# Dilated window attention with a mixture of experts on one core: where the mask's second half is loaded, three gathers instead of two at an early table, and two weight sums placed later

## The chip, the core and the metric

The kernel runs on one core of one Trainium2 chip. A core has a matrix engine (TensorE, here PE, with its weight loads shown as PEld), a vector engine (DVE), a scalar engine (ACT), a general engine (GpSimd, here POOL) and a sync engine (SyncE, here SP) that issues most of the DMA transfers. Sixteen DMA engines move the data. The metric is the device time of one execution in microseconds (us), as the median of several runs.

## The reference

Attention with a window of 32 keys for the first four heads and with 32 keys at a distance of 4 (positions 0, 4, 8, ... back) for the last four, on 8 batches, 8 heads, 576 positions and 64 features. Its output, with the heads side by side, is a token matrix of 4608 tokens by 512. Each token then goes to one of 8 experts:

```python
logits = np.einsum('bsd,de->bse', x, w_gate)
local_gate = 1.0 / (1.0 + np.exp(-np.einsum('bsd,de->bse', x, w_local).squeeze(-1)))
...
        if s == 0 or local_gate[b, s] < 0.5:
            e = fresh_e
        else:
            e = prev_e if prev_e >= 0 else fresh_e
...
        h = np.maximum(x[b, s] @ w1[e], 0.0)
        out[b, s] = p[e] * (h @ w2[e])
```

A token takes the expert with the largest logit, or the expert of the token before it where its locality gate is at least 0.5. Weights are 512 x 1024 and 1024 x 512 per expert, in 32-bit floats.

## The kernel before

**Attention.** The 64 pairs of batch and head are taken two at a time: 32 head pairs, numbered n, and their loads come for two head pairs at once, numbered m = n // 2 (16 of them). `kq` holds keys and queries of an m, `vt` its values with a column of ones. For each n, `scores(n)` computes on PE, for blocks of 64 queries, the products with the 96 keys they can see, into a score bank of which there are two; DVE (line 332) limits them from below and takes the minimum with the mask `mk`; ACT (line 335) takes the exponential. `values(n)` multiplies with `vt` on PE (line 380), and DVE divides by the sum that came out of the column of ones (lines 384 and 385), which gives `x`. `turn` transposes `x` for the router, `store` writes it to memory as `xd`, and `spread(m)` lets POOL copy the second half of a `vt` into place (line 274). The order in the loop over n is scores of n, then values of n - 1. Heads of the plain and of the dilated kind need different masks: the kind is `(n % 4) // 2`, so n = 0 and 1 use the first half of `mk`, n = 2 and 3 the second, and so on. Loads of an m are issued in the iteration n = 2(m - 2), once a buffer is free (three buffers each for `kq` and `vt`).

**Routing.** Tokens are routed in four groups of two batches. `route(g)` computes the group's logits and lays a list of small steps (expert chosen, carried from the token before, counted, position in the expert's list) into two queues, `waiting` and `behind`, from which `gap` takes one at each gap of the matrix work. After two groups an early table of tokens exists (`early_tokens`), after four the late one (`late_tokens`).

**Experts.** The work is a list of units. A pair unit has 256 tokens of one expert; units 0 and 1 use the early table, and the units from 2 on the late table. `gather(u)` lists the gathers that fetch a unit's token rows from `xd` (four for each of the units 0 to 3), `fetch` issues one: a small memset on DVE, then an indirect DMA from POOL. `turn_rows` transposes the rows, and the expert's two layers follow, `hidden(u)` and `output(u)`. A pair unit's layer is computed with seven products of quarter matrices instead of eight (unit 1's hidden layer excepted), for which DVE forms sums of the weights' quarters (`sums_of_weights`, lines 870 to 873 and 876 to 879), of token rows (`xc`) and of hidden values (`hc`). The seven products of a layer share three banks of partial sums; each is drained on ACT or DVE as it ends (`finish`, line 1119 for the second layer).

**What sets the order.** PE and DVE execute in the order in which the program writes their instructions. Work that is pushed into `soon` is taken from it one or two at a time by `work_gap`, once per product. The instructions of POOL and ACT are put in order by a planner, from the program and costs that it assumes. SP issues its transfers in the program's order and on one queue. A transfer on it carries one of eight semaphores in turn, so the ninth waits until the first has landed.

Of the kernel before, what the change touches and what calls it, by code (L numbers as in the profile page):

```python
# [12 lines left out]
BF16 = mybir.dt.bfloat16  # L13
# [3 lines left out]
Alu = mybir.AluOpType  # L17
# [6 lines left out]
B, H, S, DH = 8, 8, 576, 64  # L24
# [8 lines left out]
QB = 64  # L33
NB = S // QB
KW = QB + WIN
# [170 lines left out]
def whole(ctx, tc, exact, bad, qk, v, wgl, w1, w2, con, msk, qmk, out, cst, wg, ones):  # L206
    nc = tc.nc
    name = "exact" if exact else "plain"
# [17 lines left out]
    def room(to, i, name, shape):  # L226
# [8 lines left out]
    ins, work, xp, xtp = (attention.enter_context(tc.tile_pool(name=name, bufs=bufs))  # L235
                     for name, bufs in (("ins", 3), ("work", 3), ("xp", 3), ("xtp", 2)))
# [53 lines left out]

    load(0, "kq", 0)
    if not exact:
        mk = work.tile([KW, 2 * S], BF16, name="mk", bufs=1)
        nc.sync.dma_start(out=mk[:, :S], in_=msk[:, :S])
    else:
        qm = work.tile([P, QB + 2 * NB * KW], BF16, name="qm", bufs=1)
        nc.sync.dma_start(out=qm, in_=qmk)
# [5 lines left out]
    load(1, "vt")  # L303
    if not exact:
        nc.sync.dma_start(out=cst, in_=con)
        nc.sync.dma_start(out=mk[:, S:], in_=msk[:, S:])
    spread(0)


# [5 lines left out]
    def scores(n):  # L315

        kt, qt = keys(n)
        kind = (n % NP) // (NP // 2)
        prob[n] = []
        for part, (a, z) in enumerate(UNITS):  # L320
            w = (z - a) * QB
            sc = two("sc")
            for i in range(a, z):
                for u in range(2):
                    h = slice(u * DH, (u + 1) * DH)
                    nc.tensor.matmul(sc[:KW, u, (i - a) * QB:(i - a + 1) * QB], lhsT=kt[h, i * QB:i * QB + KW],  # L326
                                     rhs=qt[h, i * QB:(i + 1) * QB], start=True, stop=True,
                                     tile_position=(u * DH, 0))
            pr = prs[n % 2 * 2 + part]
            to = pr[:KW, :, :w]  # L330
            at = kind * S + a * QB
            nc.vector.scalar_tensor_tensor(  # L332
                to, sc[:KW, :, :w], -CEIL,
                mk[:, at:at + w].unsqueeze(1).to_broadcast([KW, 2, w]), Alu.max, Alu.min)
            nc.scalar.activation(to, to, Act.Exp, scale=SCALE)  # L335
            prob[n].append(pr)

# [369 lines left out]
    def table(late):  # L707

        cols = COLS if late else 2 * FIRST
        chosen = tiles["chosen", late]  # L710
        ep = bank([1, cols], "ep")
        for k, c in enumerate(chosen):
            nc.tensor.matmul(ep, lhsT=cst[:, C_E:C_UP], rhs=c[:, 0], start=(k == 0), stop=(k == len(chosen) - 1))
        tiles["experts", late] = experts = sm.tile([1, cols], I32, name="experts_late" if late else "experts_early")
        nc.vector.tensor_copy(experts, ep)
# [140 lines left out]
    def now(push):  # L856
        for f in push:
            f()
# [22 lines left out]
    def sums_of_weights(u, second):  # L881

        i = units[u]["slot"]
        assert (u, second) in loads
        if second:
            return sums_right(sums[1], *(quarter(raw2[i], k, j, True) for k in range(2) for j in range(2)))
        return sums_left(sums[0], *(quarter(raw1[i], f, k, False) for f in range(2) for k in range(2)))
# [242 lines left out]
    def route(g):  # L1130

        turned_back, first_best, owned, exponentials = fresh(g)
        before_it, lane_and_segment = place(g)
        lane0, lane1, segment, code, what = matrices(g)
        counts = count(g == NG - 1)

        def now(*fs):
            return [lambda: [f() for f in fs]]

        def of(*fs):  # L1140
            return [lambda: [f(g) for f in fs]]

        def sum_up():
            products(g, not g)

        def counted_on():
            next(counts)

        if g < NG - 1:
            logits(g)  # L1150
            if g == EARLY - 1:
                tail = (now(what) + now(counted_on) + now(sum_up, counted_on) + pause
                        + now(lambda: table(False), early_tokens))
            else:
                tail = now(segment, code, what) + now(lane0) + pause + now(lane1) + pause * 2 + now(sum_up)
            if g == 0:
                waiting.extend(now(turned_back) + now(first_best) + now(owned) + now(exponentials) + of(carry)
                               + pause + of(carry_over) + of(total) + of(carry_in) + pause + of(choose) + of(counted)
                               + now(before_it) + now(lane_and_segment))
            else:  # L1160
                waiting.extend(pause * (g - 1) + now(turned_back, first_best) + now(owned) + now(exponentials)
                               + of(carry) + pause + of(carry_over) + of(total) + of(carry_in) + of(choose)
                               + of(counted) + pause * (g - 1) + now(before_it))
                if g == EARLY - 1:
                    waiting.extend(now(lane_and_segment, segment, code) + now(lane0) + now(lane1))
                else:
                    waiting.extend(now(lane_and_segment))
            waiting.append(lambda: (gate(g), behind.extend(tail)))
            return
        logits(g)  # L1170
        waiting.extend(now(turned_back, first_best) + now(owned) + now(exponentials) + of(carry) + of(total)
                       + of(carry_over) + pause + of(carry_in) + of(choose) + of(counted) + now(before_it)
                       + now(lane_and_segment, segment) + now(lane0, lane1) + now(lambda: gate(g), code, what)
                       + now(counted_on) + now(sum_up, *[counted_on] * (PASSES if exact else 1)) + pause * 2
                       + now(lambda: table(True)) + now(late_tokens) + now(two_more) + now(places))

    def two_more():
        for _ in range(2):
            fetches.pop(0)[1]()

    def early_tokens():
        tokens(False)
        gather(0)
        two_more()
        since[0] = 0

    def late_tokens():
        tokens(True)
        for u in range(FIRST, TURNED):
            gather(u)  # L1190
        two_more()
        ready.add("late")
        next_weights()

    warm(9)
    for n in range(NPB + 2):
        m = n // 2 + 2
        ahead = n % 2 == 0 and m < NPB // 2
        if ahead:
            for part in (0, 1) if m == 2 else (None,):  # L1200
                load(m, "kq", part)
            if n == 2 and not exact:
                nc.sync.dma_start(out=wg.rearrange("p k e -> p (k e)"), in_=wgl)
        done = (n - 3) // 2
        if n >= 4 and n % 2 == 0:
            turn(done, 2)
        if n < NPB:
            (scores_exact if exact else scores)(n)
        if n % 2 == 0:
            gap(2)  # L1210
        if 1 <= n <= NPB:
            values(n - 1)
        if ahead:
            load(m, "vt")
        if n == NPB - 4:
            weights(0, False)
        if n % 2 and n // 2 + 1 < NPB // 2:
            spread(n // 2 + 1)
        if n >= 3 and n % 2 == 1:
            turn(done, 0)  # L1220
            gap(2)
            turn(done, 1)
        gap(2)
        if n >= 4 and n % 2 == 0 and done % (2 * GB) == 2 * GB - 1:
            route(done // (2 * GB))
        if n >= 3 and n % 2 == 1:
            store(done)
        if n == NPB - 2:
            weights(0, True)
# [42 lines left out]
    def run_hidden(u, push):  # L1272
        soon.extend(push)
        for k, fits in enumerate(hidden(u)):
            work_gap(fits, 2 if units[u]["kind"] == "pair" else 1)
            if u == FIRST and k == 1:
                early_sums[u] = sums_of_weights(u, True)
                soon.extend(early_sums[u][:2])
            if u == FIRST and k == 4:
                turn_rows(u + 1)  # L1280
        flush()
        if u < FIRST:
            next_weights((u, False))
        elif after[u] is not None:
            weights(after[u], False)
# [33 lines left out]
    features(1)  # L1319
    now(both(0))  # L1320
    run_output(0, [])
    run_hidden(1, sums_of_weights(1, True))
    now(units[1]["sums"])
    fed = False
    for k, fits in enumerate(output(1)):
        work_gap(fits)
# [97 lines left out]
```

## Time and profile before

| | |
|---|---|
| three runs | 657.4, 655.79, 654.62 us; median 655.79 |
| profiled execution | 655.5 us, span of its instructions 653.7 us, granted clock 0.992 |
| PE busy | 635.1 us (97% of the span) |
| DVE, POOL, ACT busy | 415.9, 252.5, 177.6 us |
| first score of the attention stage | 5.2 us |
| first product of unit 0 | 151.1 us |
| late table's first step on PE (`ep`) | 194.0 us |

The span begins with the first instruction; the profiled execution is 1.8 us longer than its span. A row of the timeline or the chain begins with its start and its length in us. In brackets stands how long the engine was idle before the instruction, and what ended that.

### The profile page before, as it was taken

What the parts mean: (1) busy time and instruction counts of PE and PEld (TensorE: products, weight loads), DVE (VectorE), ACT (ScalarE), POOL (GpSimd) and SP (SyncE); (2) the same over time, 40 slices, a digit from 0 to 9 for tenths busy, and PEclk for the clock granted to TensorE, in tenths of its full rate; (3) what the DMA queues carried; (4) which work ended last, traced back from release to release, by engine and by line L of the source; (5) the groups of instructions that cost most, each with busy time, mean ns of one, the idle gap of its engine ahead of it and who ended that gap; (6) DMA issues with size and microseconds to landing.
All of it is one profiled execution on the core that took longest, in us unless ns stands there. A gap on an engine that the chain in (4) does not pass through costs nothing.

```text
span 653.7 us, 14687 instructions
## 1 busy us (share of the span) xinstructions
PE 635.1 (97%) x5978; PEld 558.6 (85%) x5978; DVE 415.9 (64%) x963; ACT 177.6 (27%) x318; POOL 252.5 (39%) x242
## 2 busy tenths in 40 slices
PE   7999999999999999999999999999999999999995
PEld 6888888878888999998699998799997799997973
DVE  2777888989588495754729734739714649707450
ACT  2554544342212332112132112132122123121310
POOL 5322151224016735545746553427653443110011
PEclk9899999999999999999999999999999999999998
DMA  9999998598006697674714425544114554531201
GB/s 339 410 393 315 345 316 291 188 341 341 9 32 210 220 417 272 218 269 175 282 61 155 167 86 228 202 173 162 52 50 157 200 224 200 173 147 38 105 33 44
DMA packets 29132, 131.40 MB, mean 201 GB/s; under 512 B 4925, under 2 KB 15485, under 8 KB 23296
## 3 DMA queue, kind: packets, MB, share of 16 engines
q1 hardware_dynamic: 21312, 110.96, 46.0%
q0 software_dynamic: 7744, 19.41, 8.8%
q8 instruction: 49, 0.80, 0.5%
q14 instruction: 27, 0.22, 0.1%
HBM read 145.03 MB, written 19.40 MB: 252 GB/s over the span
## 4 chain that ended last, share of the span: by engine, by line
PE 87%; DVE 7%; DMA 3%; issue 1%; POOL 1%; ACT 0%; SPq 0%; POOLq 0%; DVEq 0%
PE yp L1104 30%; PE hp L1028 27%; PE sc L326 7%; PE pv L380 4%; PE hp L1002 4%; PE yp L1092 4%; PE yp L1075 2%; PE tp L399 2%; PE hp L990 2%; DMA mk<-in_msk_dram 2%; PE ap L615 1%; DVE pr L332 1%; DMA xd<-x 1%; DVE x L385 1%; PE lp L429 1%
## 5 line engine op out<-in xcount | busy, mean ns | idle before, releaser
L911 POOL DMA_INDIRECT xg<-xd,at x120 | 136.5, 1138 | 144.0 <-DVE xg L910 119.5
L1063 POOL DMA_INDIRECT out_dram<-y,tok x36 | 47.5, 1319 | 119.6 <-DVE y L1119 65.0
L1038 DVE TENSOR_TENSOR h<-hp,h 128x512 f32<-128x512 f32 x45 | 31.0, 690 | 93.1 <-PE hp L1028 92.9
L1104 PE MATMUL yp<-sum,hc 128*128 128x256 f32 x384 | 88.5, 380 | 0.0
L1028 PE MATMUL hp<-xc,sum 128*128 128x128 f32 x720 | 85.6, 275 | 0.0
L1028 PEld LDWEIGHTS hp<-xc,sum 128*128 128x128 f32 x720 | 82.9, 192 | 0.1
L1104 PEld LDWEIGHTS yp<-sum,hc 128*128 128x128 f32 x384 | 72.9, 190 | 9.8
L1119 DVE SCALAR_TENSOR_TENSOR y<-yp,gate,y 128x256 f32<-128x256 f32 x48 | 23.2, 484 | 76.2 <-issue 47.3
L332 DVE SCALAR_TENSOR_TENSOR pr<-sc,mk 96x512 f32<-96x512 f32 x64 | 46.8, 747 | 26.7 <-PE sc L326 20.6
L1104 PE MATMUL yp<-raw,h 128*128 128x256 f32 x256 | 61.0, 381 | 0.0
L326 PE MATMUL sc<-kq 64*96 64x64 f32 x1152 | 57.4, 252 | 3.4 <-DVE pr L332 3.2
L335 ACT ACTIVATE pr<-pr 96x512 f32<-96x512 f32 x64 | 43.8, 684 | 61.0 <-DVE pr L332 59.1
L274 POOL COPY vt<-vt 32x585 f32<-32x585 f32 x48 | 33.1, 690 | 68.9 <-DMA vt<-in_v_dram 47.2
L326 PEld LDWEIGHTS sc<-kq 64*96 64x96 f32 x1152 | 52.9, 165 | 7.8 <-DVE pr L332 3.8
L1028 PE MATMUL hp<-xe,raw 128*128 128x128 f32 x480 | 58.9, 276 | 0.7 <-ACT xe L944 0.7
L1028 PEld LDWEIGHTS hp<-xe,raw 128*128 128x128 f32 x480 | 56.5, 192 | 2.9 <-issue 1.6
L1104 PEld LDWEIGHTS yp<-raw,h 128*128 128x128 f32 x256 | 47.4, 190 | 9.0 <-issue 3.2
L1032 ACT COPY h<-hp 128x512 f32<-128x512 f32 x45 | 26.3, 585 | 74.3 <-PE hp L1028 74.3
L1039 ACT ACTIVATE h<-h 128x512 f32<-128x512 f32 x45 | 28.4, 631 | 63.1 <-DVE h L1038 52.7
L380 PE MATMUL pv<-vt,pr 128*64 128x65 f32 x1152 | 42.2, 228 | 1.9 <-issue 1.0
L380 PEld LDWEIGHTS pv<-vt,pr 128*64 128x64 f32 x1152 | 37.4, 140 | 4.3 <-issue 1.2
L1112 ACT ACTIVATE y<-yp,gate 128x256 f32<-128x256 f32 x48 | 22.7, 473 | 59.9 <-PE yp L1104 59.9
(224 smaller groups left out, 953.7 us busy)
## 6 DMA issues: line engine op xcount, KB each, us to landing
raw<-in_w_dram SPq DMA_DIRECT2D x48, 2048.0 KB
kq<-in_qk_dram SPq DMA_DIRECT2D x13, 1184.0 KB
vt<-in_v_dram SPq DMA_DIRECT2D x15, 880.0 KB
xd<-x SPq DMA_DIRECT2D x16, 512.0 KB
kq<-in_qk_dram SPq DMA_DIRECT2D x6, 592.0 KB
xg<-xd,at POOLq DMA_INDIRECT x120, 3.5
xd<-x SPq DMA_DIRECT2D x32, 32.0 KB
vt<-in_v_dram SPq DMA_DIRECT2D x1, 585.0 KB
```

The source lines that it names most:

```text
L274: nc.gpsimd.tensor_copy(t[k * WIN:(k + 1) * WIN, VQ:], t[KW:, k * NB * VW:(k + 1) * NB * VW])
L326: nc.tensor.matmul(sc[:KW, u, (i - a) * QB:(i - a + 1) * QB], lhsT=kt[h, i * QB:i * QB + KW], rhs=qt[h, i * QB:(i + 1) * QB], start=True, ...
L332: nc.vector.scalar_tensor_tensor(to, sc[:KW, :, :w], -CEIL, mk[:, at:at + w].unsqueeze(1).to_broadcast([KW, 2, w]), Alu.max, Alu.min)
L335: nc.scalar.activation(to, to, Act.Exp, scale=SCALE)
L380: nc.tensor.matmul(pv[half * QB:(half + 1) * QB, k - a], lhsT=pr[:, u, (i - a) * QB:(i - a + 1) * QB], rhs=vt[:, u, i], start=True, stop=T ...
L911: nc.gpsimd.indirect_dma_start(out=to, out_offset=None, in_=of, in_offset=bass.IndirectOffsetOnAxis(ap=place, axis=0))
L1028: nc.tensor.matmul(to[:, m], lhsT=a[:, m, kk], rhs=b[:, kk], start=first and m == 0 and kk == 0, stop=(kk == DK // 2 - 1), skip_group_chec ...
L1032: nc.scalar.copy(at((0, 1, 3)[k]), of)
L1038: nc.vector.tensor_tensor(at(k), of, at(k), op=Alu.add)
L1039: nc.scalar.activation(at(k), at(k), Act.Relu)
L1063: nc.gpsimd.indirect_dma_start(out=rows_of_out(), out_offset=bass.IndirectOffsetOnAxis(ap=of_unit(u, "tok", j), axis=0), in_=y, in_offset= ...
L1104: nc.tensor.matmul(to, lhsT=a[:, m], rhs=b[:, m], start=first and m == 0, stop=(m == FK // 2 - 1), skip_group_check=True)
```

## The change

Three things change.

First, the mask's two halves get a buffer each, `mks[0]` and `mks[1]`. The first is loaded where it was. The second is loaded in the iteration n = 2 of the attention loop, after `wg` and ahead of `scores(2)`, and no longer behind the constants `cst` ahead of the loop.

Second, `early_tokens` issues three gathers of unit 0 at once, where it was two. The late table issues two and two, as before.

Third, of the four sums of unit 1's second weights, two stay in the gaps of unit 1's hidden layer, and the other two are pushed into `soon` for the gaps of its output products.

```diff
-        mk = work.tile([KW, 2 * S], BF16, name="mk", bufs=1)
-        nc.sync.dma_start(out=mk[:, :S], in_=msk[:, :S])
+        mks = [work.tile([KW, S], BF16, name=f"mk{k}", bufs=1) for k in range(2)]
+        nc.sync.dma_start(out=mks[0], in_=msk[:, :S])
...
         nc.sync.dma_start(out=cst, in_=con)
-        nc.sync.dma_start(out=mk[:, S:], in_=msk[:, S:])
...
-            at = kind * S + a * QB
             nc.vector.scalar_tensor_tensor(
                 to, sc[:KW, :, :w], -CEIL,
-                mk[:, at:at + w].unsqueeze(1).to_broadcast([KW, 2, w]), Alu.max, Alu.min)
+                mks[kind][:, a * QB:a * QB + w].unsqueeze(1).to_broadcast([KW, 2, w]), Alu.max, Alu.min)
...
-    def two_more():
-        for _ in range(2):
+    def some(count):
+        for _ in range(count):
             fetches.pop(0)[1]()
 
     def early_tokens():
         tokens(False)
         gather(0)
-        two_more()
+        some(3)
         since[0] = 0
...
             if n == 2 and not exact:
                 nc.sync.dma_start(out=wg.rearrange("p k e -> p (k e)"), in_=wgl)
+                nc.sync.dma_start(out=mks[1], in_=msk[:, S:])
...
-    run_hidden(1, sums_of_weights(1, True))
+    seconds = sums_of_weights(1, True)
+    run_hidden(1, seconds[:2])
     now(units[1]["sums"])
+    soon.extend(seconds[2:])
```

In `late_tokens` and in `route`, `two_more` becomes `some(2)`, which is the same.

How this moves instructions is shown at three places. The first is SP's queue from the last load of m = 1 on (`vt_104`); then come `cst`, two halves of `kq` and a `vt` for m = 2, `kq` for m = 3, `wg`, and `vt` for m = 3. `DMAHW` and a number is the semaphore of an earlier transfer on this queue. Before:

```order
L268 DMA vt_104<-in_v_dram 128x1760 [waits Pool_49]
L305 DMA cst<-in_con_dram 128x599 [waits DMAHW0_49]
L306 DMA mk<-in_msk_dram 96x576 [waits DMAHW1_49]
L268 DMA kq<-in_qk_dram 128x1184 [waits DMAHW2_49]
L268 DMA kq<-in_qk_dram 128x1184 [waits DMAHW3_49]
L268 DMA vt_105<-in_v_dram 128x1760 [waits DMAHW4_49,Pool_49]
L268 DMA kq<-in_qk_dram 128x2368 [waits DMAHW5_49,PE_49]
L1203 DMA wg<-in_wg_dram 128x128 [waits DMAHW6_49]
L268 DMA vt_103<-in_v_dram 128x1760 [waits DMAHW7_49,PE_49,Pool_49]
```

And after the change:

```order
L268 DMA vt_104<-in_v_dram 128x1760 [waits Pool_49]
L305 DMA cst<-in_con_dram 128x599 [waits DMAHW0_49]
L268 DMA kq<-in_qk_dram 128x1184 [waits DMAHW1_49]
L268 DMA kq<-in_qk_dram 128x1184 [waits DMAHW2_49]
L268 DMA vt_105<-in_v_dram 128x1760 [waits DMAHW3_49,Pool_49]
L268 DMA kq<-in_qk_dram 128x2368 [waits DMAHW4_49,PE_49]
L1201 DMA wg<-in_wg_dram 128x128 [waits DMAHW5_49]
L1202 DMA mk_120<-in_msk_dram 96x576 [waits DMAHW6_49]
L268 DMA vt_103<-in_v_dram 128x1760 [waits DMAHW7_49,PE_49,Pool_49]
```

The mask's second half has gone behind five transfers, and the transfers that it passed each wait for a semaphore one earlier.

The second place is POOL's order around the first gathers (`xg`), at the end of the attention stage, with the last copies of `vt` and a product of the routing (`what`). Before:

```order
L274 COPY vt_103<-vt_103 32x585
L911 DMA xg<-xd,row_2122 128x256 [waits DMAHW0_49,DMAHW5_49,DVE_49,Pool_49]
L911 DMA xg<-xd,row_2123 128x256 [waits DVE_49]
L274 COPY vt_103<-vt_103 32x585 [waits DMASW3_49,DMASW2_49]
L911 DMA xg<-xd,row_2122 128x256 [waits DVE_49,Pool_49]
L911 DMA xg<-xd,row_2123 128x256 [waits DVE_49]
L911 DMA xg<-xd,row_2122 128x256 [waits DVE_49]
L604 TENSOR_TENSOR what<-is_it,cst 128x9x56 [waits DVE_49]
```

After:

```order
L274 COPY vt_103<-vt_103 32x585 x2
L909 DMA xg<-xd,row_2123 128x256 [waits DMAHW0_49,DMAHW5_49,DVE_49,Pool_49]
L909 DMA xg<-xd,row_2124 128x256 [waits DVE_49]
L909 DMA xg<-xd,row_2123 128x256 [waits DVE_49]
L909 DMA xg<-xd,row_2124 128x256 [waits DVE_49]
L909 DMA xg<-xd,row_2123 128x256 [waits DMASW3_49,DMASW2_49,DVE_49]
L602 TENSOR_TENSOR what<-is_it,cst 128x9x56 [waits DVE_49]
```

The last copy, which waited for the first two gathers, now stands ahead of them; that wait stands at the fifth gather, the first of unit 1. (Two copies of earlier `vt` have also moved ahead of earlier products `what` on POOL.)

The third place is DVE's order around the late table. `chosen_late` is what PE's `ep` waits for, `hc` are the sums of unit 1's hidden values, and `sum` from `raw_1` are the weight sums in question. Before:

```order
L673 TENSOR_TENSOR bef_late<-bef_late,done_early 128x8
L878 TENSOR_TENSOR sum_2507<-raw_1_2508 128x1024
L620 TENSOR_TENSOR acc<-acc,ap 112x128
...
L703 TENSOR_SCALAR chosen_late<-cst,one_late 128x48 x2
L879 TENSOR_TENSOR sum_2507<-raw_1_2508,sum_2507 128x1024
L715 CAST experts_late<-ep 1x48
L764 COPY acc<-acc 112x64
```

After, there and further on:

```order
L701 TENSOR_SCALAR chosen_late<-cst,one_late 128x48 x2
L713 CAST experts_late<-ep 1x48
L762 COPY acc<-acc 112x64
...
L871 TENSOR_TENSOR hc<-h,hc 128x512
L876 TENSOR_TENSOR sum_2508<-raw_1_2509 128x1024
L908 MEMSET xg 1x1
L738 TENSOR_SCALAR y<-fq 128x192
...
L743 SCALAR_TENSOR_TENSOR at<-y,cst 128x192
L877 TENSOR_TENSOR sum_2508<-raw_1_2509,sum_2508 128x1024
L868 TENSOR_TENSOR sum_79<-raw_0_77 128x1024
```

The second of the moved sums stood between `chosen_late` and the cast of the experts; the first stood 16 rows ahead of `chosen_late` (line 878). Both now follow the `hc` sums, one on each side of the arithmetic on `fq`.

More of the change, by code (lines that the diff above doesn't have):

```diff
@@ L1174, in route @@
                        + now(counted_on) + now(sum_up, *[counted_on] * (PASSES if exact else 1)) + pause * 2
-                       + now(lambda: table(True)) + now(late_tokens) + now(two_more) + now(places))
-    def two_more():
-        for _ in range(2):
+                       + now(lambda: table(True)) + now(late_tokens) + now(lambda: some(2)) + now(places))
+    def some(count):
+        for _ in range(count):
             fetches.pop(0)[1]()
@@ L1190, in late_tokens @@
             gather(u)
-        two_more()
+        some(2)
         ready.add("late")
```

## Prediction

> **What bounds the kernel now.** I read the page first (PE is busy 97% of the span), then the list of what PE waited for, which says what is left to win or to lose on the engine that sets the end. Columns: engine, line, what it waited for, us in total, times, longest.
>
> ```profile
> PE sc L326 <- DVE pr L332: 3.2, 1, 3.2
> ...
> PE hp L1028 <- ACT xe L944: 0.7, 1, 0.7
> ...
> PE tp L943 <- DMA xd<-x: 0.6, 1, 0.6
> PE ep L713 <- DVE chosen_late L703: 0.6, 1, 0.6
> ...
> PE sc L326 <- DMA kq<-in_qk_dram: 0.2, 1, 0.2
> ```
>
> The change touches the places of the first four rows: the 3.2 us is where the second mask half is awaited, the next two are unit 0's gathers, the fourth is the weight sums. PE as a whole waited 0.2 us for loads of q and k, once. So a delay put on PE early in the attention stage has no later wait to vanish in; that decides most of what follows.
>
> Then I read the timeline of the first 40 us around the mask (start, duration, engine, line, operation; in brackets the idle time before it and what ended it).
>
> ```profile
> 5.21 0.44 SPq L306 DMA_DIRECT2D mk<-in_msk_dram  x1
> ...
> 12.17 0.33 SPq L1203 DMA_DIRECT2D wg<-in_wg_dram  x1
> 12.98 1.15 PE L380 MATMUL pv<-vt,pr 128*64 128x65 f32 x32 [0.89 <-POOL vt L274]
> ...
> 16.58 1.42 DVE L332 SCALAR_TENSOR_TENSOR pr<-sc,mk 96x512 f32<-96x512 f32 x2 [5.59 <-DMA mk<-in_msk_dram]
> 17.32 3.15 PE L326 MATMUL sc<-kq 64*96 64x64 f32 x36 [3.19 <-DVE pr L332]
> ...
> 20.40 2.13 PE L380 MATMUL pv<-vt,pr 128*64 128x65 f32 x36
> ...
> 21.44 2.12 POOL L274 COPY vt<-vt 32x585 f32<-32x585 f32 x3 [4.01 <-DMA vt<-in_v_dram]
> ...
> 26.92 2.12 POOL L274 COPY vt<-vt 32x585 f32<-32x585 f32 x3 [3.36 <-DMA vt<-in_v_dram]
> ```
>
> The scores of head pair 2 (n=2, the first dilated one) need the mask's second half. Its load goes out at 5.21, behind everything issued before it, and ends DVE's wait at 16.58, 11.4 us later. PE ran dry at 14.13 and restarts at 17.32. The half is thus on the path already. The two POOL rows are markers of the transfers behind it: vt of m=2 has landed at 21.44, vt of m=3 at 26.92.
>
> **Edit 1, the mask's second half.** SP now issues that load after wg. Before it in the queue then stand both kq loads of m=2, vt of m=2, kq of m=3 and wg; all of them were behind it before. The two buffers add no instruction. Sizes (KB each, after the count):
>
> ```profile
> kq<-in_qk_dram SPq DMA_DIRECT2D x13, 1184.0 KB
> vt<-in_v_dram SPq DMA_DIRECT2D x15, 880.0 KB
> ...
> mk<-in_msk_dram SPq DMA_DIRECT2D x2, 108.0 KB
> wg<-in_wg_dram SPq DMA_DIRECT2D x1, 64.0 KB
> ```
>
> Between the markers the queue moved kq of m=3, wg and vt of m=3: 1184 + 64 + 880 = 2128 KB in 26.92 - 21.44 = 5.48 us, 388 KB/us. The mask, now behind wg, lands when kq of m=3 and wg have followed vt of m=2: 21.44 + 1248 / 388 = 24.66. (Its own 108 KB leave vt's front and join the end, so they cancel.) DVE's operation of n=2 moves from 16.58 to 24.66: **+8.1 us**. Bounds from the rows nearest to it: it is behind vt of m=2, so not before 21.44 - 108/388 = 21.2 (+4.6), and ahead of vt of m=3, so not after 26.92 (+10.3). I take the value between, because the queue stood full over all of it (windows below). When it is issued matters little: SP reaches it right behind wg, at 12.17 or soon after.
>
> Queued behind that DVE instruction are the reciprocals and products of n=1 and so the store of m=0; PE's scores of n=3 wait for the score bank that it frees. Does the delay stay? These windows (stretch; its length, then PE, PEld, DVE, ACT, POOL busy with counts; granted clock; DMA share; GB/s):
>
> ```profile
> 14.00:16.00 2.00, 0.13 (x6) 0.00 (x0) 0.00 (x0) 0.00 (x0) 0.67 (x1) 0.87 1.05 371
> 16.00:18.00 2.00, 0.68 (x8) 0.68 (x10) 1.42 (x3) 0.63 (x1) 1.34 (x2) 0.50 1.05 416
> ...
> 20.00:22.00 2.00, 2.00 (x36) 1.88 (x36) 1.20 (x3) 0.99 (x2) 0.56 (x1) 0.50 0.99 411
> 22.00:24.00 2.00, 2.00 (x31) 1.76 (x27) 0.91 (x3) 1.02 (x3) 1.44 (x3) 0.92 1.03 404
> ...
> 30.00:35.00 5.00, 5.00 (x113) 4.65 (x111) 3.58 (x8) 2.61 (x5) 1.49 (x3) 1.00 1.05 412
> ```
>
> From 20 us on PE shows no gap here, and SP's own list says who paces the loads:
>
> ```profile
> SPq L268 <- PE pv L380: 46.5, 14, 5.1
> ```
>
> Loads wait for PE to free buffers, 46.5 us in all, so a PE that is 8.1 us late passes it on to the loads. The clock fell to 0.50 from 16 to 22 us: that price is in the time before already, and I count it once after as well. Taken: +8.1.
>
> **Edit 2, a third gather at the early table.** Unit 0 needs four gathers. In the trace the third and fourth sit on POOL behind a copy of vt that waits for the first two:
>
> ```profile
> 141.30 0.67 POOL L274 COPY vt<-vt 32x585 f32<-32x585 f32 x1 [6.80 <-DMA xg<-xd,row]
> ...
> 143.51 0.95 POOL L911 DMA_INDIRECT xg<-xd,row  x1 [0.30 <-DVE oh L525]
> 150.00 0.44 PE L943 MATMUL tp<-cst,xg 128*128 128x128 f32 x2 [0.63 <-DMA xd<-x]
> 151.12 2.05 PE L1028 MATMUL hp<-xe,raw 128*128 128x128 f32 x16 [0.67 <-ACT xe L944]
> 160.29 0.17 DVE L475 TENSOR_TENSOR code<-code,own 128x9 f32<-128x9 f32 x1
> 160.52 0.28 PE L488 MATMUL rp<-cst,code 128*9 128x128 f32 x1
> 161.72 0.68 DVE L1038 TENSOR_TENSOR h<-hp,h 128x512 f32<-128x512 f32 x1
> 162.46 2.05 PE L1028 MATMUL hp<-xc,raw 128*128 128x128 f32 x16
> ```
>
> In the changed order all copies stand ahead of the gathers, and all four go out some 8 us sooner, so the 0.63 us in front of PE's last two transposes goes, and with it most of the 0.67 us behind (ACT's copy then follows ACT's previous one). PE would reach unit 0's products about 0.7 us sooner. But what is late next is DVE: between 147.0 and 162.4 it is busy without a pause, and two of PE's steps follow it to the tenth, rp at 160.52 behind code (ends 160.46), and the seventh product at 162.46 behind the h that ends at 162.40. The row for the stretch:
>
> ```profile
> 147.00:162.40 15.40, 14.10 (x127) 12.86 (x122) 14.97 (x35) 4.19 (x8) 5.81 (x5) 1.00 0.92 357
> ```
>
> DVE is busy 14.97 of 15.40 us, and the edit takes nothing out of it: the memset ahead of a gather (0.06 us) only moves to before the stretch. PE gains 0.7 us and gives it back at 160.5. Taken: 0; bounds -0.7 (DVE's lag is otherwise less) and +0.1 (one memset more at the early table, where DVE is on the path).
>
> **Edit 3, two weight sums moved.** The sums L878 and L879 for unit 1's output leave the routing arithmetic and stand behind the sums of hidden values. First the row of one in the chain of waits (start, length), then the timeline:
>
> ```profile
> 189.62 1.14 DVE sum L878
> ```
>
> ```profile
> 189.55 1.21 DVE L878 TENSOR_TENSOR sum<-raw 128x1024 f32<-128x1024 f32 x1
> 193.98 0.24 PE L713 MATMUL ep<-chosen_late,cst 128*1 128x48 f32 x2 [0.59 <-DVE chosen_late L703]
> ...
> 207.94 0.48 DVE L1119 SCALAR_TENSOR_TENSOR y<-yp,gate,y 128x256 f32<-128x256 f32 x1
> ...
> 209.43 0.42 DVE L876 TENSOR_TENSOR xc<-xe 128x256 f32<-128x256 f32 x1 [1.00 <-ACT xe L944]
> ...
> 210.35 1.89 PE L1104 MATMUL yp<-sum,h 128*128 128x256 f32 x8
> ```
>
> Without L878 ahead of it, chosen_late ends some 1.1 us sooner and PE's 0.59 us wait at ep goes. Both sums (2 x 1.14 us) now stand ahead of L1119 at 207.94. The seventh product of unit 1, at 210.35, writes the bank that this L1119 reads. L1119 then ends at 207.94 + 0.48 + 2.28 - 0.59 = 210.1 and PE comes for the bank at 210.35 - 0.59 = 209.76: 0.3 us of the gain goes back. The later xc at 209.43 moves into the 1.00 us that DVE idles there and is needed only by the second product after the seventh. Taken: **-0.3**; bounds -0.6 (nothing given back) and +0.1.
>
> **Sum.** 655.5 (the profiled execution) + 8.1 + 0 - 0.3 = 663.3. The median of the three runs shown is 655.79, 0.3 above that execution; I forecast **663.5 us**. With the bounds added: 655.5 + 4.6 - 1.3 = 658.8 to 655.5 + 10.3 + 0.2 = 666.0.
>
> **Rivals.** 0.5% of the time, 3.3 us, is about what a measurement of this kernel can tell from no change.
>
> *The small transfer overtakes.* If 108 KB need not wait for the megabytes ahead of them, the half lands about 3.5 us after its issue, the time of a gather by the page's list of issues:
>
> ```profile
> xg<-xd,at POOLq DMA_INDIRECT x120, 3.5
> ```
>
> 12.5 + 3.5 = 16.0, 0.6 us sooner than now: 655.5 - 0.6 - 0.3 = 654.6, not slower. Against it: in the time before the same transfer on the same queue took 11.4 us and came out behind its predecessors. 6%. [...]
>
> *The transfers pace the stage, and PE catches up.* DMA share is about 1.0 in the windows above. If so, the delay costs only the time in which DMA runs dry: vt of m=3 still lands by 26.9, and kq of m=4 goes out when the scores of n=3 end, 3.9 us after DVE's restart (17.32 + 3.15 against 16.58), at 28.6. That is 1.7 us: 655.5 + 1.7 - 0.3 = 656.9, within 0.5%. Against it stand PE's gapless windows and SP waiting for PE. 8%.
>
> *The cold clock lasts longer.* PE idles 11 us instead of 3. If the 0.50 then holds twice as long, PE loses again what it lost before. The scores of 3.15 us took, warm,
>
> ```profile
> 10.07 1.75 PE L326 MATMUL sc<-kq 64*96 64x64 f32 x36
> ```
>
> 1.4 us less; the values step at 20.40 took 2.13 us for 36 where 32 took 1.15 warm, 0.8 us more than its share of 1.29. Together 2.2 us: 665.5. 10%. [...]
>
> *The half comes before PE needs it.* If it landed by 14.1, PE's 3.19 us and the cold 2.2 us would go, with both small gains (0.7 + 0.6): 655.5 - 6.7 = 648.8. It needs a transfer that is faster than any row here; 3%.
>
> **Chances.** The forecast 73%, its range 658.8 to 666.0; longer cold clock 10%, inside it; pacing by transfers 8%; overtaking 6%; early half 3%. The range holds 83% and stays as it is. Slower by over 0.5% (above 659.1): the first two, 83%; within 0.5%: the next two, 14%; faster: 3%.
>
> **What would show it.** In the profile after: the first DVE operation with the second mask buffer starts near 24.7 with an idle time of about 13.7 us before it, ended by that load; PE's scores of n=3 near 25.4 at a clock of 0.50; from there to 140 us the same durations as before, all some 8 us later. The first two of PE's waits for gathers are gone, while rp and the seventh product of unit 0 wait for DVE; no wait at ep, a short one at the seventh product of unit 1. The forecast is wrong if the mask lands before 21, or if the end of the attention stage is late by less than the start.

## The result and the profile after

The changed kernel takes 664.24 us in the median of four runs (663.22 to 665.22), where the kernel before takes 655.20 (653.45 to 657.40, four runs beside it): a ratio of 1.0136, 95% interval 1.0100 to 1.0172. It is slower by about 9 us, as forecast (663.5, range 658.8 to 666.0). The profiled execution took 664.64 us with a span of 662.8, 9.1 us more than the span before (653.7).

First, what PE waited for in the changed kernel (engine, line, what it waited for, us in total, times, longest; `issue` is a pause in which PE waited for nothing that the profile shows):

```profile
PE sc L325 <- DVE pr L330: 12.0, 2, 11.8
PE pv L378 <- issue: 1.6, 1, 1.6
...
PE rp L486 <- DVE code L473: 0.7, 1, 0.7
```

The 3.2 us for the mask have become 11.8. The wait for unit 0's rows at `tp` (0.6) and the wait at `ep` (0.6) are gone, and a new one of 0.7 us stands at `rp`. The chain of waits (start, length, what) has this row in the place of the 11.24 us from 5.21 on:

```profile
11.83 12.92 DMA mk<-in_msk_dram
```

Then the timeline of the same stretch as before:

```profile
11.83 0.33 SPq L1202 DMA_DIRECT2D mk<-in_msk_dram  x1
...
12.64 1.15 PE L378 MATMUL pv<-vt,pr 128*64 128x65 f32 x32 [0.43 <-POOL vt L274]
...
21.05 2.12 POOL L274 COPY vt<-vt 32x585 f32<-32x585 f32 x3 [3.72 <-DMA vt<-in_v_dram]
24.88 1.42 DVE L330 SCALAR_TENSOR_TENSOR pr<-sc,mk 96x512 f32<-96x512 f32 x2 [13.77 <-DMA mk<-in_msk_dram]
...
25.62 3.14 PE L325 MATMUL sc<-kq 64*96 64x64 f32 x36 [11.83 <-DVE pr L330]
...
26.91 2.13 POOL L274 COPY vt<-vt 32x585 f32<-32x585 f32 x3 [3.74 <-DMA vt<-in_v_dram]
...
27.50 0.38 SPq L410 DMA_DIRECT2D xd<-x  x1
...
28.69 2.22 PE L378 MATMUL pv<-vt,pr 128*64 128x65 f32 x36
...
29.52 0.54 SPq L268 DMA_DIRECT2D kq<-in_qk_dram  x1
...
30.84 2.14 PE L397 MATMUL tp<-cst,x 128*128 128x128 f32 x9
...
32.91 1.75 PE L325 MATMUL sc<-kq 64*96 64x64 f32 x36
```

The second mask half lands between the two markers, vt of m=2 (21.05) and vt of m=3 (26.91), at the place in the queue where it was put. PE restarts at 25.62 and needs 7.3 us until the scores of n=4; before, that piece was 6.3 us, as the row at 23.59 shows. The kernel before, PE alone:

```profile
23.59 1.75 PE L326 MATMUL sc<-kq 64*96 64x64 f32 x36
...
43.58 0.39 PE L380 MATMUL pv<-vt,pr 128*64 128x65 f32 x5 [0.53 <-issue]
43.90 1.20 PE L399 MATMUL tp<-cst,x 128*128 128x128 f32 x9
```

The windows of the changed kernel say what clock was granted and what the DMA engines did (columns as in the prediction):

```profile
14.00:16.00 2.00, 0.00 (x0) 0.00 (x0) 0.00 (x0) 0.00 (x0) 0.74 (x2) 0.94 1.02 420
...
24.00:26.00 2.00, 0.38 (x5) 0.38 (x6) 1.12 (x2) 0.40 (x1) 0.00 (x0) 0.50 0.43 167
26.00:28.00 2.00, 2.00 (x30) 2.00 (x30) 1.93 (x6) 0.96 (x2) 1.03 (x2) 0.50 0.05 12
...
32.00:34.00 2.00, 2.00 (x31) 1.71 (x29) 0.07 (x1) 1.34 (x3) 0.00 (x0) 0.80 1.03 426
```

The queue runs dry at 26 to 28 us (12 GB/s). SP stood for 11.5 us in front of the store of m=0, until 27.50, because the store needs what DVE computes behind the mask; then it waited for PE before it issued kq of m=4 at 29.52. So the loads are put off behind DVE and PE, and do not pace the stage. The clock stays at 0.50 until about 32.8. The later places, PE and DVE of the changed kernel:

```profile
54.00 0.39 PE L378 MATMUL pv<-vt,pr 128*64 128x65 f32 x5 [1.63 <-issue]
54.31 1.20 PE L397 MATMUL tp<-cst,x 128*128 128x128 f32 x9
...
160.98 2.05 PE L1026 MATMUL hp<-xe,raw 128*128 128x128 f32 x16 [0.73 <-ACT xe L942]
...
171.18 0.28 PE L486 MATMUL rp<-cst,code 128*9 128x128 f32 x1 [0.66 <-DVE code L473]
...
203.99 0.25 PE L711 MATMUL ep<-chosen_late,cst 128*1 128x48 f32 x2
...
217.70 1.22 PE L941 MATMUL tp<-cst,xg 128*128 128x128 f32 x8
218.30 0.48 DVE L1117 SCALAR_TENSOR_TENSOR y<-yp,gate,y 128x256 f32<-128x256 f32 x1
...
218.75 1.89 PE L1102 MATMUL yp<-raw,hc 128*128 128x256 f32 x8
...
219.84 0.48 DVE L1117 SCALAR_TENSOR_TENSOR y<-yp,gate,y 128x256 f32<-128x256 f32 x1
...
220.48 1.89 PE L1102 MATMUL yp<-sum,h 128*128 128x256 f32 x8
```

Set against the same instructions before, these starts are the whole account (us):

| on PE | before | after | later by | step |
|---|---|---|---|---|
| scores of n=3 | 17.32 | 25.62 | 8.30 | +8.30 mask |
| scores of n=4 | 23.59 | 32.91 | 9.32 | +1.02 clock |
| transposes behind the `issue` pause | 43.90 | 54.31 | 10.41 | +1.09 pause, 0.53 to 1.63 |
| unit 0's first product | 151.12 | 160.98 | 9.86 | -0.80 gathers, after +0.25 on the way |
| `rp` of the last group | 160.52 | 171.18 | 10.66 | +0.80 given back |
| `ep` | 193.98 | 203.99 | 10.01 | -0.65 sums |
| unit 1's sixth output product | 208.62 | 218.75 | 10.13 | +0.12, in the transposes ahead of it |
| end of the span | 653.7 | 662.8 | 9.1 | -1.03: the last output landed sooner |

From 218.75 to PE's last product nothing moves any more.

### The profile page after: what moved, and what is told of

It is laid out like the page before. It is cut to its first block, busy times and chain, and to the rows that moved or that the text cites. A ratio compares the mean times of both kernels' runs of the same rounds, so it can differ in the third digit from the quotient of the medians.

```text
span 662.8 us, 14686 instructions
## 1 busy us (share of the span) xinstructions
PE 636.6 (96%) x5978; PEld 559.5 (84%) x5978; DVE 416.8 (63%) x963; ACT 177.8 (27%) x318; POOL 254.4 (38%) x242
## 4 chain that ended last, share of the span: by engine, by line
PE 86%; DVE 7%; DMA 4%; issue 1%; POOL 1%; ACT 0%; POOLq 0%; DVEq 0%; SPq 0%
PE yp L1102 29%; PE hp L1026 25%; PE sc L325 6%; PE hp L1000 4%; PE yp L1090 4%; PE pv L378 4%; PE tp L397 2%; PE yp L1073 2%; PE hp L988 2%; PE hp L1015 2%; DMA mk<-in_msk_dram 2%; DVE pr L330 1%; DMA kq<-in_qk_dram 1%; PE ap L613 1%; DVE x L383 1%
## 5 line engine op out<-in xcount | busy, mean ns | idle before, releaser
L1117 DVE SCALAR_TENSOR_TENSOR y<-yp,gate,y 128x256 f32<-128x256 f32 x48 | 23.2, 484 | 76.1 <-issue 47.3
```

## The experiments

Every diff is against the changed kernel. The kernel before takes another time on each of three chips that these runs had (676.80, 656.05 and 655.32 us in the median), so each ratio is to runs of the kernel before on the same chip. On the first of them the stretch from `ep` to the end of the span is 475.9 to 482.4 us long in the four traces taken there, where it is 459.7 in the kernel before and 458.8 in the changed one (in the trace with the half on POOL's queue PE idles 11.7 us in front of products of line 1026, which neither of those two does); from that chip I use the ratios and the first 30 us of the traces, and of the later rows only waits.

**The mask's move alone** (the gathers and the sums as before):

```diff
-        some(3)
+        some(2)
...
-    seconds = sums_of_weights(1, True)
-    run_hidden(1, seconds[:2])
+    run_hidden(1, sums_of_weights(1, True))
     now(units[1]["sums"])
-    soon.extend(seconds[2:])
```

> Only the first of the three edits: a buffer for each half of the mask, the second half loaded behind wg; two gathers at the early table and the weight sums where they were. Theory (the mask's place in SP's queue makes the whole loss, the two other edits are worth about -0.6 us together): the first DVE operation with the second half starts at 24.7 to 25.1 us as in the changed kernel, the products of unit 0 are some 10.5 us late, and the time is about 9.5 us above the kernel before. Rival (the other two edits, or the order on POOL that came with them, carry part of the loss): clearly less than 9 us above the kernel before.

688.18 us, ratio 1.0169 (1.0121 to 1.0216). DVE's first operation with the half starts at 24.95, as in the changed kernel, and the wait at `ep` is there as before the change:

```profile
24.95 1.42 DVE L330 SCALAR_TENSOR_TENSOR pr<-sc,mk 96x512 f32<-96x512 f32 x2 [13.69 <-DMA mk<-in_msk_dram]
...
177.18 0.28 PE L486 MATMUL rp<-cst,code 128*9 128x128 f32 x1 [0.66 <-DVE code L473]
...
210.64 0.25 PE L711 MATMUL ep<-chosen_late,cst 128*1 128x48 f32 x2 [0.59 <-DVE chosen_late L701]
```

The loss is the mask's. And `rp` waits 0.66 us here with two gathers at the early table: with the mask loaded late, POOL's order already has the copies of `vt` ahead of the gathers, so what Edit 2 was to bring is there without it.

**The other two edits alone** (the mask's second half behind `cst` again):

```diff
         nc.sync.dma_start(out=cst, in_=con)
+        nc.sync.dma_start(out=mks[1], in_=msk[:, S:])
...
-                nc.sync.dma_start(out=mks[1], in_=msk[:, S:])
```

> The changed kernel with the second half's load back at its old place behind cst (in its own buffer), so the gathers and the weight sums alone. Theory: the attention stage starts as before (DVE's first use of the second half at 16.6 us); PE's 0.6 us wait at ep is gone; unit 0 gains up to 0.8 us at its first product and loses it again at rp; time 0 to 0.7 us below the kernel before, not to be told from no change. Rival (the edits are worth more than I gave them, and the queue took it away): 1.5 us or more below.

674.60 us, ratio 0.9974 (0.9944 to 1.0003). DVE starts with the half at 16.56, PE waits at `rp` (0.66) and not at `ep`. The interval holds the forecast -0.3 us as well as no change; it excludes that these two edits cost anything like 9 us.

**The mask's second half in front**, right behind the first:

```diff
         nc.sync.dma_start(out=mks[0], in_=msk[:, :S])
+        nc.sync.dma_start(out=mks[1], in_=msk[:, S:])
...
-                nc.sync.dma_start(out=mks[1], in_=msk[:, S:])
```

> The changed kernel with the second half loaded right behind the first one, at the front of SP's queue. Theory (place in the queue is all that matters): no wait for the mask at n=2, PE goes on at 14.1 us instead of 17.3 (before) or 25.6 (after) and its clock does not fall to 0.50, so 3.2 us and up to 2.2 us of slow clock are saved; 649.5 to 652 us, 3 to 5.5 us below the kernel before. Rival (the transfers pace this stage): PE meets the next wait, for vt of m=1, whose copy on POOL ends near 17.4 us in the trace before, and little is won: 654 us or more.

672.44 us, ratio 0.9926 (0.9898 to 0.9953): 5.0 us of 676.80 faster than before, as expected. DVE starts with the half at 12.07 without a wait for it; the scores of n=3 start at 15.10, where they started at 17.32.

**The same late load, on POOL's queue instead of SP's:**

```diff
-                nc.sync.dma_start(out=mks[1], in_=msk[:, S:])
+                nc.gpsimd.dma_start(out=mks[1], in_=msk[:, S:])
```

> The changed kernel with the second half's load issued by POOL on its own queue, at about 6 us by the order of its instructions, which is about when the kernel before issued it on SP's. The megabytes in flight are the same. Theory (what delays the half is its place behind others on SP's queue): it lands within about 5 us, before n=2 needs it, and the time is that of the load at the front, 649.5 to 652 us. Rival (what delays it is the load on the DMA engines as a whole): DVE waits for it until 16 us or later, and the time is 655 us or more.

671.69 us, ratio 0.9932 (0.9905 to 0.9960). POOL issues it at 5.81:

```profile
5.81 0.56 POOL L1202 DMA_DIRECT2D mk<-in_msk_dram  x1
...
11.49 1.42 DVE L330 SCALAR_TENSOR_TENSOR pr<-sc,mk 96x512 f32<-96x512 f32 x2 [0.84 <-DMA mk<-in_msk_dram]
...
14.44 1.75 PE L325 MATMUL sc<-kq 64*96 64x64 f32 x36
```

From issue to use it takes 5.7 us, where it takes 11.4 us on SP's queue before (5.21 to 16.58) and 13.1 in the changed kernel (11.83 to 24.88). The DMA engines are as busy as before meanwhile: their share is 1.00 to 1.05 in stretches of 2 us from 6 to 12 us, in both traces. What delays the half is its place in SP's queue, not that the DMA engines are loaded.

**The half one step earlier in SP's queue**, behind vt of m=2 and ahead of kq of m=3 and wg:

```diff
         if ahead:
+            if n == 2 and not exact:
+                nc.sync.dma_start(out=mks[1], in_=msk[:, S:])
             for part in (0, 1) if m == 2 else (None,):
...
-                nc.sync.dma_start(out=mks[1], in_=msk[:, S:])
```

> The changed kernel with the mask's second half loaded one step earlier: behind vt of m=2, ahead of kq of m=3 and wg, so 1248 KB fewer stand ahead of it. Theory (it lands where the bytes ahead of it end, at 388 KB/us): the first DVE operation with it starts near 21.3, 3.2 to 3.6 us sooner than in the changed kernel (24.88) and 4.6 later than before (16.58); PE idles some 8.2 us; the transposes of n=3 and what follows come 3.3 to 4.2 us sooner than in the changed kernel, ratio to the kernel before 1.005 to 1.008. Rival (what delays it is the wait of SP or the number of transfers, not the bytes): it starts before 18 or after 24.

661.21 us, ratio 1.0084 (1.0053 to 1.0114).

```profile
21.94 1.42 DVE L330 SCALAR_TENSOR_TENSOR pr<-sc,mk 96x512 f32<-96x512 f32 x2 [10.95 <-DMA mk<-in_msk_dram]
...
22.68 3.15 PE L325 MATMUL sc<-kq 64*96 64x64 f32 x36 [9.06 <-DVE pr L330]
```

With 1248 KB fewer ahead of it, it is used 2.94 us sooner than in the changed kernel (425 KB/us; I expected 3.2 to 3.6, and 21.3). The landing follows the bytes ahead of it. PE's last product comes 4.3 us sooner than in the changed kernel; the ratio lies just above what I expected, with an interval that holds most of it.

**Keeping PE busy while it waits**, with the changed kernel itself on the same chip. The edit puts idle products of a matrix of ones behind the values of n=1 (38, and 50 in a later run); nothing computed from them is used:

```diff
         if 1 <= n <= NPB:
             values(n - 1)
+        if n == 2:
+            warm(38)
```

> The changed kernel as it is, on one chip with the three that follow, so that they can be compared with it. Theory (the delay of the mask's second half is the loss, +8.3 us, with some 2 us of cold clock and issue pauses behind it): ratio to the kernel before 1.011 to 1.017, DVE's first operation with the second half at 24.5 to 25.2, PE's transposes behind head pair 3 some 10 us later than before. Rival (the loss belongs to the first chip alone): ratio within 1.000 to 1.008.

> The changed kernel with 38 idle products of a matrix of ones put on PE between the values of n=1 and the scores of n=3, so that PE is busy over most of its wait for the mask. Nothing it computes is used. The mask comes no sooner. Theory (part of the loss is that the clock is granted at 0.50 for 7 us after the wait): with the clock at 1.00 when the scores of n=3 start, their 3.14 us become 1.75, the values 2.22 become 1.3, the nine transposes 2.07 become 1.13, so the scores of n=4 start some 3.2 us sooner than in the changed kernel and the end comes 2 to 3.2 us sooner: ratio to the kernel before about 1.009 where the changed kernel has 1.0136. Rival (the cold stretch hides beside late loads, which pace the stage): the scores of n=4 start sooner, but the gain is gone at head pair 8, and the ratio is that of the changed kernel.

> The changed kernel with 50 idle products of the matrix of ones on PE in its wait for the mask, where 38 ended 3.21 us before the mask and the clock was at 0.50 again. 100 matmuls at 0.115 us end near 25.3, just ahead of the scores. Theory (the cold clock costs what the scores, values and transposes take longer at 0.50): the clock stays at 1.00, the scores of n=4 start near 29.6, 3.3 us sooner than in the changed kernel (32.91) and 2.7 sooner than with 38 (32.34), and the end is 2 to 3.3 us sooner than in the changed kernel. Rival (the clock falls by another cause than PE's idling): the scores of n=3 take 3.14 us again.

The changed kernel again: 663.32 us, ratio 1.0111 (1.0091 to 1.0131). With 38: 662.47, 1.0110 (1.0091 to 1.0130). With 50, on the third chip: 660.30, 1.0069 (1.0048 to 1.0091). With 38, PE alone:

```profile
13.78 8.75 PE L289 MATMUL warm<-ones 128*128 128x128 f32 x76
25.74 3.14 PE L325 MATMUL sc<-kq 64*96 64x64 f32 x36 [3.21 <-DVE pr L330]
...
32.34 1.75 PE L325 MATMUL sc<-kq 64*96 64x64 f32 x36
```

The filling ended 3.21 us too early, the clock was down again (0.50 from 24.69 on), and the expected gain failed; but that gave the comparison that I lacked: 3.21 us of idling, as in the kernel before, at the changed kernel's place. It still took 6.60 us to the scores of n=4. With 50:

```profile
13.51 11.43 PE L289 MATMUL warm<-ones 128*128 128x128 f32 x100
25.75 1.80 PE L325 MATMUL sc<-kq 64*96 64x64 f32 x36 [0.81 <-DVE pr L330]
...
29.85 1.75 PE L325 MATMUL sc<-kq 64*96 64x64 f32 x36
```

At full clock (1.00 throughout) the piece takes 4.10 us, from 25.75 to 29.85. So the cold clock costs 6.27 - 4.10 = 2.2 us in the kernel before and 7.29 - 4.10 = 3.2 in the changed kernel's profile; the ratio of 1.0069 against 1.0111 or 1.0136 says 2.8 to 4.4 us for the latter, in which the `issue` pause further on is included (1.63 or 1.90 us in the changed kernel's two traces, none with the filling). The rest of its loss stays: the mask is no sooner.

Does the idle time set how long the clock stays down after the restart? From windows of half a us, in all traces in which it fell there:

| kernel | PE idle | restart | clock at 0.50 | length | restart to its end | scores n=3 to n=4 |
|---|---|---|---|---|---|---|
| gathers alone (below) | 2.51 | 17.22 | 17.97 to 21.39 | 3.42 | 4.17 | 5.60 |
| the other two edits alone | 2.97 | 17.30 | 16.37 to 23.20 | 6.83 | 5.90 | 6.66 |
| before | 3.19 | 17.32 | 15.48 to 22.30 | 6.82 | 4.98 | 6.27 |
| filled with 38 | 3.21 | 25.74 | 24.69 to 31.52 | 6.83 | 5.78 | 6.60 |
| halfway | 9.06 | 22.68 | 15.45 to 29.10 | 13.65 | 6.42 | 6.92 |
| moved weight sum (below) | 11.48 | 25.59 | 17.14 to 30.79 | 13.65 | 5.20 | 6.36 |
| mask alone | 11.80 | 25.70 | 16.07 to 33.14 | 17.07 | 7.44 | 7.34 |
| changed | 11.83 | 25.62 | 15.74 to 32.81 | 17.07 | 7.19 | 7.29 |
| changed again | 12.16 | 26.00 | 14.41 to 31.48 | 17.07 | 5.48 | 6.45 |

Not by itself: an idle time of 11.5 to 12.2 us led to pieces of 6.36, 6.45, 7.29 and 7.34 us, and one of 2.97 us to 6.66. Every stretch at 0.50 is 1, 2, 4 or 5 times 3.41 us long (3.42, 6.82 or 6.83, 13.65, 17.07). What goes with the piece is how much of the stretch is left when PE restarts. The last two columns show it: the more is left (4.17 to 7.44 us), the longer the piece (5.60 to 7.34), without an exception. What sets the start of a stretch no trace shows.

**One early weight sum of unit 0 out of DVE's full stretch:**

```diff
+            if u == 0 and k == 5:
+                soon.append(early_sums[0][1])
             if u == FIRST and k == 4:
...
-    run_hidden(0, early_sums[0][:2])
+    run_hidden(0, early_sums[0][:1])
```

> The changed kernel, with one of the two early weight sums of unit 0 (1.14 us on DVE) moved from ahead of the routing arithmetic of the last group into a gap after the seventh product of unit 0's first layer. Theory (the third gather's gain of 0.7 us is given back because DVE is busy without a pause up to rp): rp of the last group and the seventh product no longer wait for DVE (0.66 us in the changed kernel), and both come 0.6 to 0.7 us sooner against unit 0's first product. Rival (something else holds rp, such as PE's own work ahead of it): the distance from unit 0's first product to rp stays 10.2 us. In the whole time 0.7 us is a ratio of 0.001, at the edge of what five rounds tell, so the trace decides.

663.80 us, ratio 1.0113 (1.0094 to 1.0131): no different from the changed kernel on the same chip. PE alone, from unit 0's first product on:

```profile
161.11 2.05 PE L1026 MATMUL hp<-xe,raw 128*128 128x128 f32 x16 [0.73 <-ACT xe L942]
...
170.48 0.27 PE L486 MATMUL rp<-cst,code 128*9 128x128 f32 x1
...
203.18 0.25 PE L711 MATMUL ep<-chosen_late,cst 128*1 128x48 f32 x2
...
218.31 1.89 PE L1102 MATMUL yp<-raw,hc 128*128 128x256 f32 x8
```

The wait at `rp` is gone and the piece from unit 0's first product to `rp` takes 9.37 us instead of 10.20: DVE's load is what took the gathers' gain back. At `ep` the kernel is 0.81 us sooner than the changed one, at unit 1's sixth output product 0.44: nearly half is given back once more, in the eight transposes ahead of that product (1.58 us here, 1.22 in the changed kernel). Why they take longer isn't shown.

**The third gather alone** (mask and sums as before):

```diff
         nc.sync.dma_start(out=cst, in_=con)
+        nc.sync.dma_start(out=mks[1], in_=msk[:, S:])
...
-                nc.sync.dma_start(out=mks[1], in_=msk[:, S:])
...
-    seconds = sums_of_weights(1, True)
-    run_hidden(1, seconds[:2])
+    run_hidden(1, sums_of_weights(1, True))
     now(units[1]["sums"])
-    soon.extend(seconds[2:])
```

> Only the third gather at the early table; mask and weight sums as before. Theory (PE gains 0.6 to 0.7 us at unit 0's first product and gives it back at rp, which waits for DVE): no row for the gather in front of PE's first transposes of unit 0, rp waits 0.6 us for DVE, the wait of 0.6 us at ep is still there, and the ratio to the kernel before is within 0.998 to 1.002. Rival (the gain stays): no wait at rp, and ep comes 0.6 us sooner than before.

656.19 us, ratio 1.0022 (1.0006 to 1.0039), just above the 1.002 that I expected at most. What PE waited for:

```profile
PE rp L487 <- DVE code L474: 0.7, 1, 0.7
PE ep L712 <- DVE chosen_late L702: 0.6, 1, 0.6
```

No wait for rows in front of unit 0, 0.66 at `rp`, 10.19 us from unit 0's first product to `rp`: the gain of 0.80 us is there and 0.79 is given back, so nothing is won. The median is 0.9 us above the kernel before. In the profile, PE's last product is 0.82 us late; 0.56 of it is there ahead of unit 0's rows (the `issue` pause of the attention stage alone is 0.55 longer, 1.08 us) and 0.27 comes in the transposes ahead of unit 1's sixth output product. Neither is at the gather, so I don't put it down to it.

**Towards a faster kernel.** The mask in front and the moved sum together, and the mask on POOL's queue with the moved sum:

```diff
         nc.sync.dma_start(out=mks[0], in_=msk[:, :S])
+        nc.sync.dma_start(out=mks[1], in_=msk[:, S:])
...
-                nc.sync.dma_start(out=mks[1], in_=msk[:, S:])
...
-    run_hidden(0, early_sums[0][:2])
+    run_hidden(0, early_sums[0][:1])
```

> The changed kernel with the mask's second half loaded right behind the first, ahead of the rest of the queue, and with the early weight sum of unit 0 moved as in the run before. Theory (the half's place in the queue is the loss; in front it takes away the 3.2 us wait and the cold clock of the kernel before too, and the freed DVE lets the gathers' 0.7 us through): 5 to 6.5 us faster than the kernel before, ratio 0.990 to 0.993, and faster than the same without the moved sum by up to 0.7 us. Rival (the time before the first scores grows as much as is won, or the loads become the bound later in the stage): ratio 0.997 or above.

> The changed kernel with the mask's second half on POOL's queue instead of SP's, and one early weight sum of unit 0 moved from ahead of the routing arithmetic to a gap after the seventh product of its first layer. Theory (the half no longer stands behind the megabytes of SP's queue, nothing of SP's is put off by it, and the freed DVE lets the gathers' 0.7 us through): the scores of n=3 near 14.4 without a cold clock, 4.5 to 6 us faster than the kernel before at a ratio of 0.991 to 0.9935. Rival (what is won early is lost to issue pauses and waits for vt in the attention stage): ratio 0.996 or above.

653.05 us, ratio 0.9956 (0.9935 to 0.9977), and 652.58, ratio 0.9960 (0.9945 to 0.9975). Both beat the kernel before, by about 3 us, and the changed kernel by some 10, but neither by the 4.5 to 6.5 us expected. For the first, PE's rows show where it went:

```profile
5.11 1.75 PE L326 MATMUL sc<-kq 64*96 64x64 f32 x36
8.44 3.15 PE L326 MATMUL sc<-kq 64*96 64x64 f32 x36 [1.58 <-DMA kq<-in_qk_dram]
11.52 2.22 PE L379 MATMUL pv<-vt,pr 128*64 128x65 f32 x36
```

In that execution the q and k behind the mask came late, and towards the end of the pause of 1.58 us, which lasted until 8.44, a stretch at clock 0.50 began (8.36 to 15.19): the price that the mask in front should save was paid at the start. The second has no stretch at 0.50; its profiled execution (650.81, the shortest of twelve) ended PE's work 4.4 us sooner than the kernel before. What the longer ones lose, up to 655.78, isn't shown. It also met a new wait at the end of the attention stage:

```profile
139.01 1.15 PE L378 MATMUL pv<-vt,pr 128*64 128x65 f32 x32 [0.55 <-POOL vt L274]
...
146.09 0.44 PE L941 MATMUL tp<-cst,xg 128*128 128x128 f32 x2 [0.55 <-DMA xg<-xd,row]
```

With the mask off SP's late place the planner puts three gathers ahead of the last copies of `vt`, which wait for them.

## Why the prediction was right

*Edit 1, +8.1 us.* Measured 8.30: DVE's first operation at 24.88, where I had 24.66, behind kq of m=3 and wg and ahead of vt of m=3, as worked out from the two markers. The mask's move alone shows the same 24.95, the half placed 1248 KB earlier comes 2.94 us earlier, and on another queue it takes half the time of the kernel before (5.7 us from issue to use, where it took 11.4). That the delay stays until the end was right too: it is 8.3 to 10.7 us at every later place of PE, and the queue running dry at 26 to 28 us (12 GB/s) shows the loads waiting behind DVE and PE.

*The clock, counted once.* That it counts once was an estimate, which no trace had shown. The term was short by 1.02 us in the profiled execution (a piece of 7.29 us, 6.27 before). The rival "the cold clock lasts longer" had the right sign, but it put 2.2 us on the longer idle time, and the idle time alone doesn't set the piece. The two executions with 11.5 and 12.2 us of idling cost 0.1 and 0.2 us more than the kernel before, the other two 1.0 and 1.1; the piece goes with what is left of the stretch at 0.50 when PE restarts, and that differs between executions of the same kernel (7.19 us left and a piece of 7.29 us; 5.48 and 6.45). That the longer idle time adds nothing at all, nine stretches can't show.

*Not in the sum: the `issue` pause.* At the same instruction of the attention stage PE pauses 0.53 us before and 1.63 after. The other traces with the mask's half behind wg have 2.73 (mask alone), 1.90 (the changed kernel again) and 1.08 (moved weight sum) there, the two fillings and the half one step earlier none, and those with the half loaded early 0.81 (three) or 1.08 (three). So it varies between kernels and runs by more than the 1.1 us in question. That the late half makes it longer is possible; what PE waits for there no trace names, and it stays open.

*Edit 2, 0.* Right, and by the mechanism named: PE gains 0.80 us at unit 0's first product and loses 0.80 at `rp`, which waits 0.66 us for DVE. Taking one weight sum out of DVE's stretch removed that wait. One thing I had not separated: either edit brings the 0.8 us by itself, the mask's move by way of POOL's order (two gathers, no wait for rows) and the third gather with the mask where it was. Unit 0's seventh product, which I expected to wait for DVE as well, shows no wait.

*Edit 3, -0.3.* Measured -0.65 at `ep`, where the wait went as predicted. The give-back was to come at unit 1's seventh product, and it did not: L1117 ends there at 219.84 + 0.48 = 220.32, ahead of PE at 220.48, so DVE was not as late against PE as I had worked out. The 0.12 us that PE loses one product earlier are not the price of the sums either. They arise in the eight transposes of token rows ahead of it, and the same eight took 1.09 us before, 1.22 in the changed kernel and 1.36 with the gathers alone, where no sum was moved:

```profile
208.25 1.36 PE L942 MATMUL tp<-cst,xg 128*128 128x128 f32 x8
```

With the other two edits alone, the sums moved, they took 1.04. With the mask on POOL's queue and the moved sum, PE waits 0.19 us there for a gather to land; what it waits for in the changed kernel no trace names. So the step of Edit 3 that failed is the 0.3 us given back; the runs show none.

*Sum.* 7.8 us forecast against 9.1 in the profiles and 7.3 to 9.0 by the medians on two chips. The terms that were missing (1.02 clock, 1.09 pause, 0.25 on the way) and the one of the other sign (-1.03, the last output landing sooner) are of the size by which executions of one kernel differ (663.22 to 665.22 us in the changed kernel's four). That the sum came within 1.3 us is in part luck: 2.4 us were missing from it, and 1.0 came off at the end in that one execution. Of the rivals, the overtaking transfer, the early half and the stage paced by transfers are excluded by the rows at 24.88 and by the delay after 54 us, which stays between 9.8 and 10.7 us.

## What to carry to other kernels

The load of 108 KB that gates an engine here landed when the bytes ahead of it in its queue had gone: sorted behind 1248 KB more it was used 2.94 us later (24.88 against 21.94), and in front of them, or on a queue with little ahead of it, it was there by 12.07 and 11.49. Where one engine sets the end and waits for nearly nothing (PE, busy 96% of the changed kernel's span), a delay early in the program stays to the last microsecond: 8.30 us at the scores of n=3 were 9.1 at the end. A gain in front of an engine that another busy engine holds up a little later is no gain until that one is relieved too: PE's 0.80 us were given back at `rp`, and with one weight sum less on DVE the piece to `rp` took 9.37 us instead of 10.20.

## What was not expected of the hardware

- Every stretch at a clock of 0.50 is 1, 2, 4 or 5 times 3.41 us long: all that the table lists, and those at 8.36 to 15.19 (mask in front and moved sum), 55.37 to 62.20 (changed again) and 57.03 to 63.86 us (mask alone). From the restart of PE to full clock it took 4.2 to 7.4 us in the table's stretches.
- Such a stretch also began with or soon after a pause far shorter than 3.41 us: 1.58 us in front of the second scores with the mask in front and the moved sum, and an `issue` pause of 1.90 us in the changed kernel again, which then ran at 0.50 from 55.37 to 62.20 in its profiled execution (669.42). After one of 1.63 us in the changed kernel none began.
- The lengths of the `issue` pause at one and the same instruction (0.53, 0.81, 1.08, 1.63, 1.90, 2.73 us) differ by about 0.27 us or multiples of it.
